# Forming Q from two absolute values of h, in a linear attention with a rational feed-forward layer

## The chip, the cores and the metric

One Trainium2 chip, one of its cores, one launch. The metric is the device time of an execution in microseconds (us). The median of three runs of the kernel before is 860.86 us (860.64 to 860.94).

## The reference

The attention is linear and its output is normalised over each head; the result, laid out as 4608 tokens of 512 features, goes through a feed-forward layer with a rational activation:

```
kv[d, e] = sum over s of k[s, d] * v[s, e]      (8 batches, 8 heads, 576 x 64)
out = q @ kv;  x = out / rms(out) * g_norm                          (4608 x 512)
h   = x @ w_in                                                      (4608 x 2048)
P   = a0 + a1 h + a2 h^2 + a3 h^3
Q   = 1 + |b0| |h| + |b1| h^2
y   = (P / (Q + 1e-6)) @ w_out                                      (4608 x 512)
```

The weights come as 64-bit floats and are taken apart on the chip.

## The kernel before

**Tiling.** The tokens are worked on in nine tiles of 512 (t = 0 to 8), the 2048 hidden features in sixteen chunks of 128 (c = 0 to 15). One pair (t, c) is a slot. In a slot TensorE (PE) makes h of a chunk, 128 x 512, in one PSUM bank (`gemm1`, L493, and L486 in the first four slots), and multiplies the activated chunk of two slots earlier with w_out (`gemm2`, L560, and L553 in the first twelve slots) into four accumulators `acc`. From tile 1 on each product is split in three fp32r matmuls of high and low parts, so a slot has 12 matmuls of `gemm1` and 12 of `gemm2`. Two PSUM banks hold h, and h of slot i+1 is made while slot i is activated.

**Activation of a slot.** It is spread over three engines, each of which runs its list in order. ScalarE (ACT): `v = |b1 h|` (L501), `u = -(a3 h + a2)` (L502), then the high part `gh` of the slot before (L539), the absolute value `q = |q|` (L510), Ln (L513) and Exp (L514), which give the first guess `r` of 1/Q in PSUM. VectorE (DVE): `q = (v + |b0|) h` (L504), `u = u h` (L505), `u = (u - a1) h` (L511), `u = (u - a0) r` (L520), `r = (q + 1 + eps) r` (L521), and the product of the Newton step with the numerator (L529). GpSimd (POOL): the low part `gl` (L540). `h` and `r` lie in PSUM; `v`, `q`, `u`, `gh` and `gl` lie in SBUF. [...]

**What else runs on these engines.** In tile 0 the weights are converted in the gaps: `hi`, `lo` (L209 on ACT, L211 on DVE), `shift` (L232), `or` (L237), `add` (L242, mostly POOL), `cast` (L249) and `rest` (L269). A table `first_tiles` written by hand names the engine, slot and place of each step; the places are points of the slot's code (s, h, q, v, e, r, g, z). From tile 1 on the attention of the next tile runs in fixed slots: `ql` on POOL (L361) in slots 3, 4, 5 and 7, its norm on POOL (L439) in slots 12 and 13, the split of the next x in slot 14 (casts L249 on ACT, low parts L316 on DVE). At the end of a tile `evacuate` copies the accumulators (L567, L569). Slot 15 of tile 8 is done in two halves by `finish`.

**Order.** The instructions are in the order in which the program is written; the framework adds the semaphore waits. It lets one engine at a time use a PSUM bank: L504, which reads h from its bank, comes after both reads of that bank by ACT (L501 and L502).

Of the kernel before, what the change touches and what calls it, by code (L numbers as in the profile page):

```python
# [12 lines left out]
AF = mybir.ActivationFunctionType  # L13
ALU = mybir.AluOpType
# [9 lines left out]
def linear_attention_then_rational_ffn(  # L24
# [10 lines left out]
    PE, ACT, DVE, POOL = nc.tensor, nc.scalar, nc.vector, nc.gpsimd  # L35
# [29 lines left out]
    b0abs = const.tile([P, 1], F32, name="b0abs")  # L65
# [46 lines left out]
    def f32(t):  # L112
        return t.bitcast(F32)
# [134 lines left out]
    def copy(by, to, of):  # L248
        ACT.copy(to, of) if by == ACT else by.tensor_copy(to, of)  # L249
# [222 lines left out]
    def strands(f):  # L472
        return f.rearrange("p (a b) -> p b a", a=2)

    def gemm1(t, c):
        if t == NTILE - 1 and c % 3 == 2:
            ph = ps_at.tile([P, TW], F32, tag="at", name=f"h_{t}_{c}", bufs=1)
        else:
            ph = ps_h.tile([P, TW], F32, tag="h", name=f"h_{t}_{c}")
        gemm1_part(t, c, ph)  # L480
        return ph
# [14 lines left out]
    def ew_a(t, c, ph, w=TW, between=lambda: None):  # L496
        nm = f"{t}_{c}"
        v = work.tile([P, w], F32, tag="d", name=f"v_{nm}")
        q = work.tile([P, w], F32, tag="q", name=f"q_{nm}")
        u = work.tile([P, w], F32, tag="u", name=f"u_{nm}")  # L500
        ACT.activation(v, ph, AF.Abs, scale=b1)  # L501
        ACT.activation(u, ph, AF.Identity, bias=na[:, 2:3], scale=na[:, 3:4])  # L502
        between()
        DVE.scalar_tensor_tensor(q, v, b0abs, ph, ALU.add, ALU.mult)  # L504
        DVE.tensor_tensor(u, u, ph, ALU.mult)  # L505
        pend[t, c] = (q, u)

    def ew_b(t, c, ph, r, between=lambda: None):
        q, u = pend[t, c]
        ACT.activation(q, q, AF.Abs)  # L510
        DVE.scalar_tensor_tensor(u, u, na[:, 1:2], ph, ALU.add, ALU.mult)  # L511
        between()
        ACT.activation(r, q, AF.Ln, bias=bias[:, 2:3], scale=QSC)  # L513
        ACT.activation(r, r, AF.Exp, bias=bias[:, 3:4], scale=-1.0)  # L514
        pend[t, c] = (q, u, r)
# [16 lines left out]
    def ew_d(t, c, w=TW):  # L532
        u = pend.pop((t, c))[1]
        if (t, c) in gs:
            return
        nm = f"{t}_{c}"
        gh = work.tile([P, w], F32R, tag="gh", name=f"gh_{nm}")
        gl = work.tile([P, w], F32R, tag="gl", name=f"gl_{nm}")
        ACT.copy(gh, u)  # L539
        POOL.tensor_tensor(gl, u, f32(gh), ALU.subtract)  # L540
        gs[t, c] = (gh, gl)
# [4 lines left out]
    def gemm2(t, c):  # L546
        g = gs.pop((t, c))
        first, last = c == 0, c == NF - 1
        if first:
            acc[t] = [ps_acc.tile([P, DM], F32, tag="acc", name=f"acc_{t}_{s}") for s in range(NSUB)]  # L550
        if unsplit2(t, c):
            for s in range(NSUB):
                PE.matmul(acc[t][s], g[:, s * P:(s + 1) * P], w32["wo", c], start=first, stop=last)  # L553
            return
        (gh, gl), (wh, wl) = g, whl["wo", c]
        products = (gh, wh), (gh, wl), (gl, wh)
        order = in_turn(behind2.get((t, c)), NSUB)
        for n, (s, j) in enumerate(order):
            a, w = products[j]
            PE.matmul(acc[t][s], a[:, s * P:(s + 1) * P], strands(w) if t else w, start=first and j == 0, stop=last and all(k != s for k, _ in order[n + 1:]))  # L560
# [14 lines left out]
    def finish(t, ph):  # L575
        c = NF - 1
        parts = [slice(k * TW // 2, (k + 1) * TW // 2) for k in range(2)]
        rooms = ("d", 2), ("q", 2), ("u", 2), ("gh", 2), ("gl", 2)
        spare = ("qr", 1), ("qh", 1), ("ql", 1), ("rb", 2), ("rb", 2)
        halves = []  # L580
        for n, tags in enumerate((rooms, spare)):
            new = [work.tile([P, TW // 2], F32 if m < 3 else F32R, tag=tag, name=f"{'vquab'[m]}_last_{n}", bufs=bufs) for m, (tag, bufs) in enumerate(tags)]
            halves.append((*new, ps_at.tile([P, TW // 2], F32, tag=("r", "at")[n], name=f"r_last_{n}", bufs=1)))
        for k, (v, q, u, gh, gl, r) in zip(parts, halves):
            ACT.activation(v, ph[:, k], AF.Abs, scale=b1)
            ACT.activation(u, ph[:, k], AF.Identity, bias=na[:, 2:3], scale=na[:, 3:4])
        ew_d(t, c - 1)
        for k, (v, q, u, gh, gl, r) in zip(parts, halves):
            DVE.scalar_tensor_tensor(q, v, b0abs, ph[:, k], ALU.add, ALU.mult)
            DVE.tensor_tensor(u, u, ph[:, k], ALU.mult)  # L590
            DVE.scalar_tensor_tensor(u, u, na[:, 1:2], ph[:, k], ALU.add, ALU.mult)
            ACT.activation(q, q, AF.Abs)
            ACT.activation(r, q, AF.Ln, bias=bias[:, 2:3], scale=QSC)
            ACT.activation(r, r, AF.Exp, bias=bias[:, 3:4], scale=-1.0)
        gemm2(t, c - 2)
        for v, q, u, gh, gl, r in halves:
            DVE.scalar_tensor_tensor(u, u, na[:, 0:1], r, ALU.add, ALU.mult)
            DVE.scalar_tensor_tensor(r, q, QEPS, r, ALU.add, ALU.mult)
            DVE.scalar_tensor_tensor(u, r, 2.0, u, ALU.subtract, ALU.mult)
            ACT.copy(gh, u)  # L600
            DVE.tensor_tensor(gl, u, f32(gh), ALU.subtract)

        def products(c, gs, order, s0=0):
            wh, wl = whl["wo", c]
            for s, j in order:
                a, w = ((gs[0], wh), (gs[0], wl), (gs[1], wh))[j]
                PE.matmul(acc[t][s], a[:, (s - s0) * P:(s - s0 + 1) * P], strands(w), start=False, stop=c == NF - 1 and j == 2)

        def store(s, by):
            ob = work.tile([P, DM], F32, tag="at", name=f"ob_{t}_{s}", bufs=4)  # L610
            r0 = t * TW + s * P
            if by is not None:
                copy(by, ob, acc[t][s])
                nc.sync.dma_start(out[r0:r0 + P], ob)
                return
            for e, (by, queue) in enumerate(((DVE, nc.sync), (ACT, ACT))):
                es = slice(e * DM // 2, (e + 1) * DM // 2)
                copy(by, ob[:, es], acc[t][s][:, es])
                queue.dma_start(out[r0:r0 + P, es], ob[:, es])

        before = gs[t, c - 1]
        products(c - 1, before, [(s, j) for s in range(2) for j in range(3)])
        products(c, halves[0][3:5], [(s, j) for s in range(2) for j in range(2)] + [(s, 2) for s in range(2)])
        store(0, DVE)
        store(1, ACT)
        for s, by in (2, DVE), (3, None):
            products(c - 1, before, [(s, j) for j in range(3)])
            products(c, halves[1][3:5], [(s, j) for j in range(3)], 2)
            store(s, by)
# [166 lines left out]
    ph = h00  # L796
# [22 lines left out]
    for i, (t, c) in enumerate(slots[:-1]):  # L819
        rest = {0: [], 1: [], 2: []}  # L820
        todo(i, "s")
        ew_a(t, c, ph, between=lambda: todo(i, "h"))
        if i:
            ew_d(*slots[i - 1])
        todo(i, "q")
        ew_b(t, c, ph, r_bank(t, c), lambda: todo(i, "v"))
        todo(i, "e")
        if i >= LAG:
# [3 lines left out]
        if i < 4:  # L832
            ph = gemm1(0, i + 1)
# [13 lines left out]
        if t == NTILE - 1:  # L847
            ahead += [gemm1(*slots[k]) for k in ((i + 1, i + 2) if c == 0 else (i + 2,)) if k < len(slots)]
            ph = ahead.pop(0) if ahead else None
        elif i >= 4:  # L850
            ph = gemm1(*slots[i + 1])
        if c == NF - 2 and 0 < t < NTILE - 1:
            xl = [split(t + 1, p) for p in range(NPAIR)]
            for k in range(2):
                rest[k].append(xl[k])
                rest[2].append(xl[2 + k])
        ew_c(t, c, lambda k: [todo(i, "rgz"[k]), *(f() for f in rest[k])])
    finish(NTILE - 1, ph)


# [42 lines left out]
```

## Time and profile before

| | us |
|---|---|
| median of three runs | 860.86 |
| the profiled execution | 860.87 |
| its span, first to last instruction | 859.1 |
| PE busy | 841.8 (98%) |
| DVE busy | 685.1 (80%) |
| ACT busy | 698.9 (81%) |
| POOL busy | 327.9 (38%) |

The page gives busy time by engine and by line. Matmul ends are modelled, so where a time lost on PE is wanted it is read from the starts: twelve matmuls of 128x512 start 0.216 us apart, 2.59 us together, and what two neighbours lie further apart is lost. The chain of waits tells which work ended last, followed back from the end. The granted TensorE clock is at its full level through the kernel.

### The profile page before, as it was taken

The numbers are of one execution on the slowest core, as the hardware profiler recorded it, in microseconds if no ns is written. First come the engines' busy times: TensorE is split into PE (matmuls) and PEld (weight loads), VectorE is DVE, ScalarE is ACT, GpSimd is POOL, SyncE is SP. The second block draws the span as 40 slices with busy tenths as digits, with TensorE's granted clock in tenths as the row PEclk, the third lists the DMA queues.
The fourth block names the chain that finished last, engine by engine and source line by source line (L and its number), as shares of the span: only waits on it lengthen the run. The fifth ranks groups of instructions, "written<-read, shape, count | busy, mean of one in ns | idle before, by whom it ended". The sixth has DMA issues, their size and how long they took to land.

```text
span 859.1 us, 11993 instructions
## 1 busy us (share of the span) xinstructions
PE 841.8 (98%) x4370; PEld 695.4 (81%) x4370; DVE 685.1 (80%) x1022; ACT 698.9 (81%) x1129; POOL 327.9 (38%) x265
## 2 busy tenths in 40 slices
PE   8999999999999999999999999999999999999997
PEld 5465568888888888888888888888888888888886
DVE  3999999987886788768875897678867877787886
ACT  5999789887798678867886888777887888778875
POOL 3596574434342143324242424233323324242221
PEclk9999999999999999999999999999999999999999
DMA  9683353023020501032113111020202010101001
GB/s 361 276 308 130 127 171 111 26 75 122 2 71 29 169 6 62 26 135 50 49 37 136 50 50 36 15 51 2 74 25 50 2 62 25 43 8 50 1 1 49
DMA packets 24191, 65.93 MB, mean 77 GB/s; under 512 B 2372, under 2 KB 2756, under 8 KB 24132
## 3 DMA queue, kind: packets, MB, share of 16 engines
q1 hardware_dynamic: 23968, 65.04, 22.4%
q8 instruction: 34, 0.56, 0.3%
q14 instruction: 25, 0.20, 0.1%
q10 hardware_dynamic: 164, 0.14, 0.0%
HBM read 55.59 MB, written 9.57 MB: 76 GB/s over the span
## 4 chain that ended last, share of the span: by engine, by line
PE 47%; DVE 26%; ACT 21%; issue 3%; DMA 2%; POOL 1%; ACTq 0%; DVEq 0%; POOLq 0%
PE h L493 21%; PE acc L560 20%; DVE u L520 5%; ACT r L513 5%; ACT q L510 5%; ACT r L514 5%; DVE q L504 5%; DVE r L521 4%; DVE u L529 4%; DVE x L316 2%; DMA raw_wi<-in_w_in_dram 2%; PE ms L344 1%; ACT u L502 1%; ACT v L501 1%; PE op L391 1%
## 5 line engine op out<-in xcount | busy, mean ns | idle before, releaser
L493 PE MATMUL h<-x,wiparts 128*128 128x512 f32 x1680 | 390.1, 382 | 0.2 <-DVE x L316 0.2
L493 PEld LDWEIGHTS h<-x,wiparts 128*128 128x128 f32 x1680 | 315.1, 189 | 50.2 <-issue 3.4
L540 POOL TENSOR_TENSOR gl<-u,gh 128x512 fp32r<-128x512 f32 x131 | 170.7, 1303 | 409.7 <-ACT gh L539 338.5
L520 DVE SCALAR_TENSOR_TENSOR u<-u,na,r 128x512 f32<-128x512 f32 x143 | 106.7, 746 | 82.0 <-ACT r L514 81.7
L504 DVE SCALAR_TENSOR_TENSOR q<-v,b0abs,h 128x512 f32<-128x512 f32 x143 | 106.1, 742 | 53.3 <-ACT u L502 52.6
L501 ACT ACTIVATE v<-h,b 128x512 f32<-128x512 f32 x143 | 98.3, 687 | 48.5 <-PE h L493 46.5
L560 PE MATMUL acc<-woparts,gh 128*128 128x512 f32 x400 | 121.1, 382 | 3.8 <-ACT r L514 2.5
L560 PE MATMUL acc<-woh,gh 128*128 128x512 f32 x320 | 121.3, 379 | 0.0
L560 PE MATMUL acc<-woh,gl 128*128 128x512 f32 x320 | 121.3, 379 | 0.0
L510 ACT ACTIVATE q<-q 128x512 f32<-128x512 f32 x143 | 90.4, 632 | 37.1 <-DVE q L504 35.3
L560 PE MATMUL acc<-wol,gh 128*128 128x512 f32 x320 | 118.9, 379 | 0.4 <-POOL wol L269 0.4
L539 ACT CAST gh<-u 128x512 fp32r<-128x512 f32 x131 | 81.1, 619 | 46.2 <-DVE u L529 46.2
L511 DVE SCALAR_TENSOR_TENSOR u<-u,na,h 128x512 f32<-128x512 f32 x143 | 106.9, 748 | 5.1
L502 ACT ACTIVATE u<-h,na 128x512 f32<-128x512 f32 x143 | 110.9, 776 | 0.0
L513 ACT ACTIVATE r<-q,bias 128x512 f32<-128x512 f32 x143 | 99.1, 693 | 4.5
L521 DVE SCALAR_TENSOR_TENSOR r<-q,r 128x512 f32<-128x512 f32 x143 | 98.5, 689 | 0.0
L514 ACT ACTIVATE r<-r,bias 128x512 f32<-128x512 f32 x143 | 94.7, 662 | 4.6
L505 DVE TENSOR_TENSOR u<-u,h 128x512 f32<-128x512 f32 x143 | 97.4, 681 | 0.0
L529 DVE SCALAR_TENSOR_TENSOR u<-r,u 128x512 f32<-128x512 f32 x131 | 90.5, 691 | 4.2
L560 PEld LDWEIGHTS acc<-woparts,gh 128*128 128x128 f32 x400 | 74.9, 189 | 17.5 <-ACT r L514 4.3
L560 PE MATMUL acc<-woparts,gl 128*128 128x512 f32 x200 | 77.2, 386 | 2.6 <-POOL gl L540 2.5
L560 PEld LDWEIGHTS acc<-wol,gh 128*128 128x128 f32 x320 | 60.5, 189 | 9.3 <-POOL wol L269 0.8
(140 smaller groups left out, 873.4 us busy)
## 6 DMA issues: line engine op xcount, KB each, us to landing
kvm<-in_kv_dram SPq DMA_DIRECT2D x28, 640.0 KB
raw_wo<-in_w_out_dram SPq DMA_DIRECT2D x8, 1024.0 KB
qr<-in_qT_dram SPq DMA_DIRECT2D x32, 256.0 KB
rb<-rd SPq DMA_DIRECT2D x32, 256.0 KB
out_dram<-ob SPq DMA_DIRECT2D x16, 512.0 KB
raw_wi<-in_w_in_dram SPq DMA_DIRECT2D x6, 1024.0 KB
first<-in_first_dram SPq DMA_DIRECT2D x4, 640.0 KB
raw_wi<-in_w_in_dram SPq DMA_DIRECT2D x4, 512.0 KB
```

The lines of the kernel that those rows point to most:

```text
L493: PE.matmul(ph, w, f, start=(n == 0), stop=(n == len(order) - 1))
L502: ACT.activation(u, ph, AF.Identity, bias=na[:, 2:3], scale=na[:, 3:4])
L504: DVE.scalar_tensor_tensor(q, v, b0abs, ph, ALU.add, ALU.mult)
L510: ACT.activation(q, q, AF.Abs)
L511: DVE.scalar_tensor_tensor(u, u, na[:, 1:2], ph, ALU.add, ALU.mult)
L513: ACT.activation(r, q, AF.Ln, bias=bias[:, 2:3], scale=QSC)
L514: ACT.activation(r, r, AF.Exp, bias=bias[:, 3:4], scale=-1.0)
L520: DVE.scalar_tensor_tensor(u, u, na[:, 0:1], r, ALU.add, ALU.mult)
L521: DVE.scalar_tensor_tensor(r, q, QEPS, r, ALU.add, ALU.mult)
L529: DVE.scalar_tensor_tensor(g, r, 2.0, u, ALU.subtract, ALU.mult)
L540: POOL.tensor_tensor(gl, u, f32(gh), ALU.subtract)
L560: PE.matmul(acc[t][s], a[:, s * P:(s + 1) * P], strands(w) if t else w, start=first and j == 0, stop=last and all(k != s for k, _ in order ...
```

## The change

ACT writes `|h|` into `q` straight from the bank of h, as the second of now three reads of that bank; DVE then forms `q = (v + |b0|) |h|` with both operands in SBUF; the absolute value of the quadratic term between DVE's step and Ln is gone. The number of instructions on each engine stays. In the slots:

```diff
         ACT.activation(v, ph, AF.Abs, scale=b1)
+        ACT.activation(q, ph, AF.Abs)
         ACT.activation(u, ph, AF.Identity, bias=na[:, 2:3], scale=na[:, 3:4])
         between()
-        DVE.scalar_tensor_tensor(q, v, b0abs, ph, ALU.add, ALU.mult)
+        DVE.scalar_tensor_tensor(q, v, b0abs, q, ALU.add, ALU.mult)
         DVE.tensor_tensor(u, u, ph, ALU.mult)
         pend[t, c] = (q, u)
 
     def ew_b(t, c, ph, r, between=lambda: None):
         q, u = pend[t, c]
-        ACT.activation(q, q, AF.Abs)
         DVE.scalar_tensor_tensor(u, u, na[:, 1:2], ph, ALU.add, ALU.mult)
```

The same in `finish`, for each half of the last slot:

```diff
             ACT.activation(v, ph[:, k], AF.Abs, scale=b1)
+            ACT.activation(q, ph[:, k], AF.Abs)
             ACT.activation(u, ph[:, k], AF.Identity, bias=na[:, 2:3], scale=na[:, 3:4])
...
-            DVE.scalar_tensor_tensor(q, v, b0abs, ph[:, k], ALU.add, ALU.mult)
+            DVE.scalar_tensor_tensor(q, v, b0abs, q, ALU.add, ALU.mult)
...
-            ACT.activation(q, q, AF.Abs)
```

ACT in slot 1 of tile 4, before (a name is tile of memory, token tile, chunk and a number; `h_4_1` is the bank of h):

```order
L501 ACTIVATE v_4_1_3895<-h_4_1_3879,b1_85 128x512
L502 ACTIVATE u_4_1_3897<-h_4_1_3879,na_83 128x512
L539 CAST gh_4_0_3902<-u_4_0_3853 128x512
L510 ACTIVATE q_4_1_3896<-q_4_1_3896 128x512
L513 ACTIVATE r_4_1_3906<-q_4_1_3896,bias_91 128x512
L514 ACTIVATE r_4_1_3906<-r_4_1_3906,bias_91 128x512
```

and now:

```order
L501 ACTIVATE v_4_1_3895<-h_4_1_3879,b1_85 128x512
L502 ACTIVATE q_4_1_3896<-h_4_1_3879 128x512
L503 ACTIVATE u_4_1_3897<-h_4_1_3879,na_83 128x512
L539 CAST gh_4_0_3903<-u_4_0_3853 128x512
L513 ACTIVATE r_4_1_3907<-q_4_1_3896,bias_91 128x512
L514 ACTIVATE r_4_1_3907<-r_4_1_3907,bias_91 128x512
```

The absolute value moved from behind `gh` to between `v` and `u`; Ln now follows `gh` and waits for DVE's q itself.

DVE from the end of slot 6 to slot 7 of tile 0, before (`wiw`, `wow`, `raw` and `wiparts` are weights under conversion, in SBUF):

```order
L237 SCALAR_TENSOR_TENSOR wiw10_638<-raw_wi10_494,wiw10_638 128x1024
L529 SCALAR_TENSOR_TENSOR g_0_6_673<-r_0_6_633,u_0_6_627 128x512
L504 SCALAR_TENSOR_TENSOR q_0_7_678<-v_0_7_677,b0abs_84,h_0_7_657 128x512
L505 TENSOR_TENSOR u_0_7_679<-u_0_7_679,h_0_7_657 128x512
L511 SCALAR_TENSOR_TENSOR u_0_7_679<-u_0_7_679,na_83,h_0_7_657 128x512
L269 TENSOR_TENSOR wiparts0_675<-wiw0_220,wiparts0_675 128x1024
```

and now:

```order
L237 SCALAR_TENSOR_TENSOR wiw10_638<-raw_wi10_494,wiw10_638 128x1024
L529 SCALAR_TENSOR_TENSOR g_0_6_673<-r_0_6_634,u_0_6_627 128x512
L505 SCALAR_TENSOR_TENSOR q_0_7_678<-v_0_7_677,b0abs_84,q_0_7_678 128x512
L506 TENSOR_TENSOR u_0_7_679<-u_0_7_679,h_0_7_657 128x512
L511 SCALAR_TENSOR_TENSOR u_0_7_679<-u_0_7_679,na_83,h_0_7_657 128x512
L269 TENSOR_TENSOR wiparts0_675<-wiw0_220,wiparts0_675 128x1024
```

Nothing moved on DVE: the second operand of q is in SBUF where it was in PSUM, and the wait for ACT's `u` went from q to the instruction behind it. POOL's list is the same as before.

## Rows read from the trace of the kernel before

**Rows 1.** Busy us by stretch: length, then PE, PEld, DVE, ACT, POOL.
```profile
31.70:134.20 102.50, 98.80 (x480) 61.23 (x479) 99.50 (x129) 92.03 (x141) 69.60 (x43) 1.00 0.50 178
...
204.00:214.00 10.00, 9.62 (x45) 8.12 (x44) 8.37 (x15) 8.12 (x15) 5.57 (x5) 1.00 0.34 91
230.00:240.00 10.00, 9.39 (x43) 7.62 (x42) 9.13 (x15) 8.62 (x14) 2.57 (x2) 1.00 0.07 25
321.00:331.00 10.00, 9.17 (x42) 7.43 (x41) 9.12 (x15) 8.50 (x14) 2.57 (x2) 1.00 0.06 21
...
684.00:694.00 10.00, 8.80 (x40) 7.09 (x39) 8.03 (x12) 8.93 (x16) 2.57 (x2) 1.00 0.05 21
430.00:462.00 32.00, 32.00 (x159) 28.16 (x157) 23.66 (x35) 27.83 (x46) 12.00 (x10) 1.00 0.12 34
```

**Rows 2.** Timeline of PE, tile 4's start and the end: start, us, idle before.
```profile
413.46 0.59 PE L560 MATMUL acc<-woparts,gh 128*128 128x512 f32 x2
414.40 0.48 PE L560 MATMUL acc<-woparts,gl 128*128 128x512 f32 x1 [0.34 <-POOL gl L540]
...
416.66 2.75 PE L493 MATMUL h<-x,wiparts 128*128 128x512 f32 x12
419.90 0.67 PE L560 MATMUL acc<-woparts,gh 128*128 128x512 f32 x2 [0.48 <-ACT r L514]
...
850.81 1.13 PE L607 MATMUL acc<-woparts,a_last 128*128 128x512 f32 x4 [0.36 <-ACT a_last L600]
```

**Rows 3.** The chain that ended last, one slot of that start.
```profile
412.27 0.66 DVE q L504
...
417.12 0.67 DVE q L504
```

**Rows 4.** Groups by line, whole kernel: busy, mean ns | idle before.
```profile
L504 DVE SCALAR_TENSOR_TENSOR q<-v,b0abs,h 128x512 f32<-128x512 f32 x143 | 106.1, 742 | 53.3 <-ACT u L502 52.6
L505 DVE TENSOR_TENSOR u<-u,h 128x512 f32<-128x512 f32 x143 | 97.4, 681 | 0.0
L510 ACT ACTIVATE q<-q 128x512 f32<-128x512 f32 x143 | 90.4, 632 | 37.1 <-DVE q L504 35.3
L394 ACT ACTIVATE sq<-op 128x512 f32<-128x512 f32 x32 | 18.9, 590 | 0.0
```

**Rows 5.** Timeline of DVE and POOL, tile 0, then before tile 4.
```profile
44.42 2.45 DVE L237 SCALAR_TENSOR_TENSOR wiw<-raw_wi,wiw 128x1024 int32<-128x1024 int32 x1
...
43.24 2.37 POOL L269 TENSOR_TENSOR wiparts<-wiw,wiparts 128x1024 fp32r<-128x1024 f32 x1 [1.44 <-ACT wiparts L249]
...
406.13 1.28 DVE L316 TENSOR_TENSOR x<-xf,x 128x512 fp32r<-128x512 f32 x2
...
406.99 1.56 POOL L540 TENSOR_TENSOR gl<-u,gh 128x512 fp32r<-128x512 f32 x1 [5.17 <-ACT gh L539]
```

**Rows 6.** Groups of DVE from 31.7 to 134.2 us; L237's spread.
```profile
L504 DVE SCALAR_TENSOR_TENSOR q<-v,b0abs,h 128x512 f32<-128x512 f32 x15 | 11.2, 746 | 0.8 <-ACT u L502 0.6
...
L237 DVE SCALAR_TENSOR_TENSOR wiw<-raw_wi,wiw 128x1024 int32<-128x1024 int32 x6 | 9.7, 1616 | 0.0
L237 DVE SCALAR_TENSOR_TENSOR wow<-raw_wo,wow 128x1024 int32<-128x1024 int32 x7 | 9.5, 1356 | 0.0
...
L237 DVE SCALAR_TENSOR_TENSOR wow<-raw_wo,wow x8: 1193/1225/1683, 26.1 to 120.8; 128x1024 int32<-128x1024 int32 x8
```

**Rows 7.** Timeline of tile 0: POOL and q, first and last meeting.
```profile
34.38 2.42 POOL L242 TENSOR_TENSOR wiw<-wiw,raw_wi 128x1024 int32<-128x1024 int32 x1 [1.22 <-issue]
...
34.68 0.75 DVE L504 SCALAR_TENSOR_TENSOR q<-v,b0abs,h 128x512 f32<-128x512 f32 x1 [0.43 <-ACT u L502]
...
122.81 2.94 POOL L242 TENSOR_TENSOR wow<-wow,raw_wo 128x1024 int32<-128x1024 int32 x1 [1.56 <-ACT raw_wo L209]
...
125.38 0.74 DVE L504 SCALAR_TENSOR_TENSOR q<-v,b0abs,h 128x512 f32<-128x512 f32 x1
```

**Rows 8.** Waits of PE from 31.7 to 134.2 us.
```profile
PE acc L560 <- POOL gl L540: 1.0, 1, 1.0
```

## The prediction

> **What bounds the kernel now.** I read three views in this order: busy time by stretch, the timeline of PE, and the chain of waits. PE is busy 98% of the span (the table above), and in the middle of a tile it has no gap at all: 32.00 of 32.00 us from 430 to 462 [rows 1]. There the activation has time to spare, and a shorter activation is worth nothing. PE loses time in two kinds of places only.
>
> The first is tile 0, from 31.7 to 134.2 us: DVE is busy 99.5 of 102.5 us, ACT 92.0, POOL 69.6, PE 98.8 [rows 1]. Four engines are nearly full, DVE most of all. What DVE loses there comes out at the end of the stretch, where PE takes up the split product of slot 12 and stands 1.0 us for its low part [rows 8].
>
> The second is the start of each of the tiles 2 to 7, six places. At tile 4 the matmul of 413.46 has a successor due 0.43 us later that starts at 414.40, a loss of 0.51; the twelve from 416.66 end at 419.25 and the next starts at 419.90, a loss of 0.65 [rows 2]. Together 1.16 us, where busy time shows 0.83 (the stretch of tile 3 has 9.17 of 10 like that of tile 4). Adding the same 0.33 to the first (0.61) and the last (1.20) of the six [rows 1] gives 0.94 + 4 x 1.16 + 1.53 = 7.1 us in all. Besides these, 0.4 us go before 214 us [rows 1] and 0.4 at the very end [rows 2]. At a tile's start the chain runs round a loop: DVE's q at 412.27, ACT's absolute value, Ln, Exp, three DVE steps, the next q at 417.12 [rows 3], 4.85 us a slot. PE needs 24 x 0.216 = 5.18, so the loop only catches up slowly with what the split of x has delayed.
>
> **The change part by part.** *ACT.* 143 absolute values of 0.632 us out of SBUF go, as many out of PSUM come. The nearest row without a scale operand that reads PSUM is the square L394, 0.590 [rows 4]. The saving of 143 x 0.04 = 6 us of ACT time lies beside fuller engines; I count nothing.
>
> *The loop.* The new absolute value runs while the previous slot is still on DVE, so a link of 0.632 [rows 4] and a hop between engines, some 0.65, leaves the loop: 4.85 becomes 4.2. DVE's own six steps, at about 0.7 each like the two of [rows 4], need 4.2 as well, so DVE is next and nothing shorter is to be had. In the middle of a tile q gains nothing: v, |h|, then q, Ln takes as long from h as v, u, q, absolute value, Ln did less some 0.1, and PE is the bound.
>
> *What the six starts get back.* The slots before them follow h of PE until slot 14, so the lead at slot 14 is one link, some 0.7 us, not several. Then the operand of q counts. gl of that slot is asked for at 406.99 and the two DVE subtractions L316 run till 407.41; POOL ends at 408.55, 1.56 after its start and 1.14 after L316's end [rows 5]. So an operation of DVE with two SBUF operands and one of POOL do not run at once. The new q, which follows L316, has two SBUF operands too, finds POOL waiting and stands some 1.1 us until gl is done. Of the lead 0.15 is left for the first wait; the next two slots win 0.65 again, which is all of the second wait. So 0.8 of 1.16 comes back, 5.0 of 7.1 over the six, with 3.9 (the second wait alone, 6 x 0.65) and 7.1 as bounds. The 0.4 before 214 and the 0.4 at the end I count as won, since nothing but the loop stands before them: **5.8 us gained from tile 1 on**, between 3.9 and 7.9.
>
> *What tile 0 pays.* The strongest row is L237: two SBUF operands, begun at 44.42 while POOL ran from 43.24 to 45.61, it took 2.45 us [rows 5] where the median is 1.22 [rows 6]. It did nothing until POOL had finished. q with h from PSUM never does that: 15 in this stretch took 0.746 on the mean, as everywhere, under POOL or not [rows 6, 4]. From now on it does. At the places where q stands now it meets a running operation of POOL eight times in this stretch. The first is 34.68 against 34.38 to 36.80, a rest of 2.1; the last is 125.38 against 122.81 to 125.75, a rest of 0.4 [rows 7]; in between the rests are 0.3, 0.6, 1.8, 0.7, 1.2 and 1.2. The sum is 8.3 us. Four more times POOL starts while q runs and is held for half of q's 0.746 on the mean, an estimated 1.5 in all, which the next DVE operation of that kind or PE's weights see. Against this, q no longer waits for u (0.8 [rows 6]), and the loop gives one link of 0.65 in slot 14: 1.5 back. The sum is 8.3 + 1.5 - 1.5 = **8.3 us lost**.
>
> The lower bound is the rate of L237 itself: 6 at 1.616 and 7 at 1.356 are 3.3 us above 13 x 1.22 [rows 6], 0.25 each; 16 q make 4.0, less 1.5 is 2.5. The upper bound adds the meeting of slot 0, before the stretch, an estimated 2.3 us, the longest rest there could be of such an operation: 10.6. I take 8.3, from the row nearest to it, q's own places: L237's successor on POOL is mostly its own consumer, so POOL stands idle when it starts; q has no such relation. Whatever DVE is late at slot 12 PE is late too, since it already stands there [rows 8].
>
> [...]
>
> The sum is made against the profiled execution, 860.87 us (span 859.1), which is also the median: 860.87 + 8.3 - 5.8 = **863.4**.
>
> **The rivals.** *Few meetings.* When q moves, it and POOL may find an order in which they miss each other as L237 mostly does. For it: the median of L237, 1.22 [rows 6], is its lone time. Then 860.87 + 2.5 - 5.8 = 857.6. *Meetings feed each other.* A held POOL operation delivers its weights late, the next DVE step meets the following one, and slot 0 starts it 2.3 us late; at the tile starts only the second wait goes: 860.87 + 10.6 - 3.9 = 867.6. POOL's 69.6 of 102.5 busy speaks for it. *The late activation is covered in tile 0.* PE has 3.7 us of idle there, and some of the delay may fall into it; with 5.8 lost and 5.8 won the time stays at 860.9. Against it: that idle exists because PE waits for the same activation. *The change does what it is written for and q is not held at all.* Then tile 0 wins 1.5, the starts 7.9: 851.5. Only the lack of a row of exactly this form speaks for it.
>
> **How the numbers follow.** A difference of 0.2%, 1.7 us, is about what a measurement of this kernel can tell from none. Chances: forecast 0.47 (861 to 866), few meetings 0.23, feeding each other 0.15, covered 0.10, not held 0.05. Faster takes few meetings nearly whole and not held: 0.27. Same takes covered and the low edge of the forecast: 0.23. Slower is the rest, 0.50. The range of 856.5 to 868.5 leaves out not held, the lower part of few meetings and the upper of feeding: 2 in 10. The likeliest case's own range is 861 to 866.
>
> **What would show it.** Right: in tile 0 q has a mean well above 0.746 with single ones of 2 to 3 us, each ending some 0.7 after a POOL operation; PE reaches the first split product later; in the tile starts the loop is 4.2, L520 waits little for Exp, gl's wait of PE is near 0.35 and the one after it is gone. Wrong: q at 0.74 throughout (then it is not held), or tile 0 of the old length with long q (then PE's slack covered it), or PE's two waits at the tile starts unchanged (then the loop was not what they wait for).

## The result and the profile after

| | before | after |
|---|---|---|
| median, four runs each on one chip (us) | 860.9 (860.64 to 861.31) | 869.28 (868.78 to 869.63) |
| ratio, 95% interval | | 1.0096 (1.0080 to 1.0112) |
| the profiled execution, its span | 860.87, 859.1 | 868.78, 867.0 |

The changed kernel is slower by 1.0%. The forecast had the side (863.4, slower the likeliest) and too little of it; the time lies 0.8 us above its range of 856.5 to 868.5.

The page of after, beside the table of before (span, busy us by engine, the chain that ended last, and the line of q):

```profile
span 867.0 us, 11988 instructions
...
PE 841.9 (97%) x4370; PEld 697.3 (80%) x4370; DVE 712.3 (82%) x1022; ACT 669.0 (77%) x1129; POOL 331.0 (38%) x265
...
PE 75%; DVE 19%; issue 2%; ACT 2%; POOL 1%; DVEq 0%; ACTq 0%; POOLq 0%
...
L505 DVE SCALAR_TENSOR_TENSOR q<-v,b0abs,q 128x512 f32<-128x512 f32 x143 | 127.0, 888 | 81.0 <-ACT q L502 81.0
```

The chain of before:

```profile
PE 47%; DVE 26%; ACT 21%; issue 3%; DMA 2%; POOL 1%; ACTq 0%; DVEq 0%; POOLq 0%
```

ACT lost 29.9 us of busy time and DVE, whose list has not changed by one instruction, gained 27.2. The chain tells that the change did in the tiles what it is for (ACT's share fell from 21% to 2%, PE's rose from 47% to 75%), so the question is where DVE's 27 us lie. q has 20.9 of them (127.0 against 106.1 [rows 4]): 10.2 in tile 0, 7.2 in the slots 15 of seven tiles, 2.8 in four slots of tile 1. A meeting, from here on, is a q that finds an operation of POOL running. What each stage makes of the time is in the next table. The first row gives when PE starts h of a slot before; the others how much later (+) or earlier (-) it starts in another kernel, each in its profiled execution. Between slot 9 of tile 1 and slot 9 of tile 7 lie the six tile starts; the kernels below "after" are the experiments.

| us | (1, 9) | (7, 9) | (8, 15) | end of span |
|---|---|---|---|---|
| before | 183.24 | 728.63 | 841.22 | 859.09 |
| after | +13.09 | +7.44 | +7.44 | +7.90 |
| `tile0_operand` | +16.07 | +16.00 | +16.00 | +16.01 |
| `tile0_order` | +0.54 | +0.49 | +0.49 | +0.49 |
| `late_only` | -0.68 | -6.28 | -6.28 | -5.82 |
| `before_small_add` | -0.85 | -0.88 | -0.88 | -0.88 |
| `after_small_add` | +3.07 | -2.68 | -2.68 | -2.21 |
| `slot0_old` | +13.99 | +8.43 | +8.43 | +8.90 |
| `five_old` | +5.66 | +0.20 | +0.20 | +0.67 |
| `order_late` | -0.91 | -10.01 | -10.01 | -9.54 |
| `late_finish_old` | -1.09 | -6.59 | -6.59 | -7.23 |
| `late_15old` | -0.98 | -9.00 | -9.00 | -9.64 |
| `abs_in_psum` | -0.93 | -10.19 | -10.19 | -10.82 |

So after pays 13.1 us ahead of slot 9 of tile 1, wins 5.65 back at the six starts, and pays 0.46 at the very end. `late_only`, with the old form in tile 0, is 0.68 early at slot 9 of tile 1; so tile 0 by itself pays some 13.8.

**Tile 0.** Groups of DVE's instructions in tile 0 (busy us, mean ns), first after, 26 to 148 us:

```profile
L505 DVE SCALAR_TENSOR_TENSOR q<-v,b0abs,q 128x512 f32<-128x512 f32 x16 | 22.1, 1384 | 0.0
L237 DVE SCALAR_TENSOR_TENSOR wow<-raw_wo,wow 128x1024 int32<-128x1024 int32 x8 | 12.8, 1602 | 0.1
...
L232 DVE TENSOR_SCALAR wow<-raw_wo 128x1024 int32<-128x1024 int32 x8 | 9.5, 1183 | 0.0
...
L237 DVE SCALAR_TENSOR_TENSOR wiw<-raw_wi,wiw 128x1024 int32<-128x1024 int32 x6 | 8.3, 1378 | 0.0
L232 DVE TENSOR_SCALAR wiw<-raw_wi 128x1024 int32<-128x1024 int32 x6 | 6.9, 1149 | 0.0
...
L242 DVE CUSTOM_DVE_ANT_0 wow<-raw_wo,wow 128x2048 uint16<-128x2048 uint16 x1 | 2.2, 2172 | 0.0
```

and the same instructions before, 26 to 135 us:

```profile
L504 DVE SCALAR_TENSOR_TENSOR q<-v,b0abs,h 128x512 f32<-128x512 f32 x16 | 11.9, 745 | 0.8 <-ACT u L502 0.6
...
L237 DVE SCALAR_TENSOR_TENSOR wow<-raw_wo,wow 128x1024 int32<-128x1024 int32 x8 | 10.7, 1340 | 0.1
L237 DVE SCALAR_TENSOR_TENSOR wiw<-raw_wi,wiw 128x1024 int32<-128x1024 int32 x6 | 9.7, 1616 | 0.0
...
L232 DVE TENSOR_SCALAR wow<-raw_wo 128x1024 int32<-128x1024 int32 x8 | 8.2, 1029 | 0.0
L232 DVE TENSOR_SCALAR wiw<-raw_wi 128x1024 int32<-128x1024 int32 x6 | 5.5, 920 | 0.0
...
L242 DVE CUSTOM_DVE_ANT_0 wow<-raw_wo,wow 128x2048 uint16<-128x2048 uint16 x1 | 1.5, 1482 | 0.0
```

q has gained 10.2 us, L232 2.7, L237 0.7 and L242 0.7: 14.3. DVE's waits ahead of slot 15 fell by 1.4 (0.8 for `u`, 0.6 for Exp), which leaves 12.9; q of slot 15 of tile 0 starts at 144.76, where it stood at 131.76. How a single q looks (start, us, [idle before <-releaser]): DVE, POOL and PE of after in slot 0:

```profile
28.07 2.89 DVE L505 SCALAR_TENSOR_TENSOR q<-v,b0abs,q 128x512 f32<-128x512 f32 x1
30.89 0.67 DVE L506 TENSOR_TENSOR u<-u,h 128x512 f32<-128x512 f32 x1
31.66 0.75 DVE L511 SCALAR_TENSOR_TENSOR u<-u,na,h 128x512 f32<-128x512 f32 x1
32.33 1.55 DVE L232 TENSOR_SCALAR wiw<-raw_wi 128x1024 int32<-128x1024 int32 x1
...
27.69 2.73 POOL L242 TENSOR_TENSOR wow<-wow,raw_wo 128x1024 int32<-128x1024 int32 x1 [3.01 <-ACT q L502]
30.36 2.98 POOL L316 TENSOR_TENSOR x<-xf,x 128x512 fp32r<-128x512 f32 x2
...
32.47 3.70 PE L486 MATMUL h<-xf,wiw 128*128 128x512 f32 x8 [2.66 <-DVE u L511]
```

q begins 0.4 us behind the start of POOL's L242, which ends at 30.42; q ends at 30.96 and is 2.89 long instead of 0.74. PE stands 2.66 for the step behind it, where it stood 0.5 before. L232 then begins under POOL's next operation and takes 1.55, where one that met nothing takes 0.69. The sixteen q of tile 0 show long ones in slots 0 (2.89), 2 (2.87), 7 (2.59), 8 (2.63) and 13 (1.75), 0.93 to 1.19 in four more, and 0.72 to 0.75 in the other seven. Each of the nine long ones ends 0.55 behind the end of a POOL operation that was running when it began.

**The tile starts.** Timeline of after at the start of tile 4 (the first pieces lie in slot 15 of tile 3): DVE, POOL, PE.

```profile
416.69 1.28 DVE L316 TENSOR_TENSOR x<-xf,x 128x512 fp32r<-128x512 f32 x2
417.90 1.77 DVE L505 SCALAR_TENSOR_TENSOR q<-v,b0abs,q 128x512 f32<-128x512 f32 x1
...
423.15 0.74 DVE L505 SCALAR_TENSOR_TENSOR q<-v,b0abs,q 128x512 f32<-128x512 f32 x1
...
427.38 0.74 DVE L505 SCALAR_TENSOR_TENSOR q<-v,b0abs,q 128x512 f32<-128x512 f32 x1
...
417.85 1.27 POOL L540 TENSOR_TENSOR gl<-u,gh 128x512 fp32r<-128x512 f32 x1 [4.99 <-ACT gh L539]
...
424.43 0.59 PE L560 MATMUL acc<-woparts,gh 128*128 128x512 f32 x2
425.36 0.48 PE L560 MATMUL acc<-woparts,gl 128*128 128x512 f32 x1 [0.33 <-POOL gl L540]
...
427.62 2.75 PE L493 MATMUL h<-x,wiparts 128*128 128x512 f32 x12
430.21 0.60 PE L560 MATMUL acc<-woparts,gh 128*128 128x512 f32 x2
```

The loop is 4.23 (423.15 to 427.38) instead of 4.85 [rows 3]. The second wait of [rows 2] is gone: 430.21 follows its twelve matmuls without a gap. The first stands nearly as it was, 0.50 lost for 0.51: q of slot 15 finds gl running and takes 1.77, 1.03 too long.

**The end.** The last slot in two halves, after:

```profile
854.57 1.28 POOL L540 TENSOR_TENSOR gl<-u,gh 128x512 fp32r<-128x512 f32 x1 [3.90 <-ACT gh L539]
854.69 1.44 DVE L590 SCALAR_TENSOR_TENSOR q_last<-v_last,b0abs,q_last 128x256 f32<-128x256 f32 x1
...
858.72 1.13 PE L607 MATMUL acc<-woparts,a_last 128*128 128x512 f32 x4 [0.83 <-ACT a_last L600]
```

The second half's q meets gl (1.44; the first half's took 0.47), and PE loses 0.99 from start to start ahead of `a_last`, where it lost 0.52 before.

### The profile page after: what moved, and what is told of

The parts are those of the page before. It is cut to its first block, busy times and chain, and to the rows that moved or that the text cites. A ratio compares the mean times of both kernels' runs of the same rounds, so it can differ in the third digit from the quotient of the medians.

```text
span 867.0 us, 11988 instructions
## 1 busy us (share of the span) xinstructions
PE 841.9 (97%) x4370; PEld 697.3 (80%) x4370; DVE 712.3 (82%) x1022; ACT 669.0 (77%) x1129; POOL 331.0 (38%) x265
## 4 chain that ended last, share of the span: by engine, by line
PE 75%; DVE 19%; issue 2%; ACT 2%; POOL 1%; DVEq 0%; ACTq 0%; POOLq 0%
PE h L493 34%; PE acc L560 33%; DVE q L505 4%; DVE u L520 2%; DVE u L511 2%; DVE x L316 2%; DVE r L521 2%; DVE u L506 2%; PE ms L344 1%; DVE wow L237 1%; DVE u L529 1%; PE op L391 1%; PE op L390 1%; PE acc L553 1%; PE ms L410 1%
## 5 line engine op out<-in xcount | busy, mean ns | idle before, releaser
L493 PE MATMUL h<-x,wiparts 128*128 128x512 f32 x1680 | 390.9, 383 | 1.6 <-ACT r L514 1.6
L493 PEld LDWEIGHTS h<-x,wiparts 128*128 128x128 f32 x1680 | 316.1, 190 | 52.1 <-issue 2.7
L505 DVE SCALAR_TENSOR_TENSOR q<-v,b0abs,q 128x512 f32<-128x512 f32 x143 | 127.0, 888 | 81.0 <-ACT q L502 81.0
L502 ACT ACTIVATE q<-h 128x512 f32<-128x512 f32 x143 | 84.8, 593 | 0.0
```

Source lines behind the costliest of these rows:

```text
L493: PE.matmul(ph, w, f, start=(n == 0), stop=(n == len(order) - 1))
L505: DVE.scalar_tensor_tensor(q, v, b0abs, q, ALU.add, ALU.mult)
```

## The experiments

**Theory:** from now on q has two operands in SBUF and cannot run while POOL works (2.89 for 0.74 in slot 0); that costs in tile 0 and nowhere else but at slot 15 and the last slot. **Rivals:** ScalarE's moved absolute value, which puts casts and conversions of tile 0 later, costs it; or what the starts win is only the catching up of a late tile 0. Line numbers shift by a few in these kernels; names don't. Each ratio in this section is against runs of the kernel before on the same chip (860.57 to 860.59 us).

### The operand alone, in tile 0

```diff
-        DVE.scalar_tensor_tensor(q, v, b0abs, ph, ALU.add, ALU.mult)
+        DVE.scalar_tensor_tensor(q, v, b0abs, ph if t else v, ALU.add, ALU.mult)
```

> The kernel before, with one difference in tile 0: q multiplies by v, in SBUF, where it multiplied by h in PSUM (so Q of tile 0 has another factor); ScalarE's absolute value stays between q and Ln, and no instruction moves. If the place of the operand is what costs in tile 0, the time is 860.9 + 13 = 874, give or take 2, and q of tile 0 shows single ones of 2 to 3 us. If the moved absolute value is what costs (three reads of h ahead of DVE, casts and conversions later on ScalarE), it is 860.9.

875.73 us against 860.59, ratio 1.0175 (1.0162 to 1.0188). Its q of tile 0, and the same group of the next kernel, in which only ScalarE's order is new:

```profile
L504 DVE SCALAR_TENSOR_TENSOR q<-v,b0abs 128x512 f32<-128x512 f32 x16 | 25.5, 1592 | 0.0
```

```profile
L506 DVE SCALAR_TENSOR_TENSOR q<-v,b0abs,h 128x512 f32<-128x512 f32 x16 | 11.9, 746 | 0.3 <-ACT u L504 0.2
```

### ScalarE's order alone, in tile 0

```diff
         ACT.activation(v, ph, AF.Abs, scale=b1)
+        if t == 0:
+            ACT.activation(q, ph, AF.Abs)
...
-        DVE.scalar_tensor_tensor(q, v, b0abs, ph, ALU.add, ALU.mult)
+        DVE.scalar_tensor_tensor(q, v, b0abs, ph, ALU.add, ALU.mult if t else ALU.max)
...
-        ACT.activation(q, q, AF.Abs)
+        if t:
+            ACT.activation(q, q, AF.Abs)
```

> The kernel before, with one difference in tile 0: ScalarE makes the absolute value of h into q between v and u, as in the changed kernel, and none between q and Ln, but VectorE's q still reads h from PSUM (it takes the larger of v + |b0| and h, so that Ln has a positive argument; Q of tile 0 is another). If the operand is what costs, there is nothing to lose here: 860.9, at best 1.5 less for the shorter loop. If the moved absolute value is what costs, 874.

861.22, ratio 1.0007 (0.9998 to 1.0015): no change. The pair settles tile 0: the operand alone costs all of it and more, the order alone nothing that can be told from none.

### The new form from tile 1 on

```diff
-        ACT.activation(q, ph, AF.Abs)
+        if t:
+            ACT.activation(q, ph, AF.Abs)
...
-        DVE.scalar_tensor_tensor(q, v, b0abs, q, ALU.add, ALU.mult)
+        DVE.scalar_tensor_tensor(q, v, b0abs, q if t else ph, ALU.add, ALU.mult)
...
+        if not (t):
+            ACT.activation(q, q, AF.Abs)
```

> The new form of q in tiles 1 to 8 and in the last slot; tile 0 as it was before. The theory (q with two operands in SBUF cannot run beside POOL, and only tile 0 has POOL busy enough for that to cost) puts +13.1 us of the traced delay into tile 0 and -5.2 behind it, so it expects 869.3 - 13.1 = 856.2 us, 4.7 under the kernel before. If what is won at the tile starts is won only because tile 0 ended late (work that had piled up by then is caught up later in any case), it is 860 to 861. If the two stages are independent but the end alone loses 1.2, its tile starts read as in the changed kernel: one wait of 0.5 for gl, none for Exp.

854.67, ratio 0.9931 (0.9920 to 0.9943), 1.5 better than expected. The starts win 5.6 here (-0.68 to -6.28 in the table) as in after (13.09 to 7.44, 5.65), so they owe nothing to a late tile 0. The two parts add up to within 1 us: `tile0_operand` with +15.1 and this with -5.9 make +9.2, and after has +8.4.

### Is it POOL's running operation?

POOL's adds on 32 columns, in either kernel:

```diff
         w = ups[u].bitcast(I32)[:, part]
+        if by == POOL:
+            w, low = w[:, 0:32], low[:, 0:32]
         by.tensor_tensor(w, w, low, ALU.add)
```

> The kernel before with POOL's adds of the weights (L242 on POOL, 34 of its 70 us in tile 0) on 32 columns of 512 or 1024 alone, so the weights lack part of their low word; nothing else is left out and no instruction moves. It is the base line for the next run: the same edit in the changed kernel. By itself it should be some 2 to 4 us under 860.9, since VectorE's L232 and L237, which stand behind such adds in tile 0 (0.69 alone, up to 1.53 beside one), become free.

> The changed kernel with the same edit. Of the 10.2 us by which q of tile 0 is too long, 7.2 stand behind an add of POOL (slots 0, 2, 3, 7, 9, 14), and so do five of the seven long L232. If POOL's running operation is what holds q, the tile 0 loss of 13 falls to 3 or 4 and this kernel is 1 to 2 us under its base line, instead of 8.4 over it; q of slots 0, 2 and 7 is 0.75. If q is slow in tile 0 for another reason (its operand, ScalarE's order, the clock), it stays 8 over the base line.

860.01, ratio 0.9993 (0.9984 to 1.0002), and 859.53, ratio 0.9987 (0.9977 to 0.9996). Of the changed form's 8.4 us -0.5 is left, and up to slot (1, 9) 3.9 of 13.1 (+3.07 less -0.85), as expected. q of slots 0, 2 and 7 is 0.74 to 0.75. But the total came out higher than the 1 to 2 us gain that I named, and the long q are not those that were left over: new ones stand in slots 3, 4 and 6, which had none or a small one (2.32, 2.85 and 1.55), behind POOL's `rest`. POOL and then DVE in slot 4:

```profile
55.79 3.50 POOL L271 TENSOR_TENSOR wiparts<-wiw,wiparts 128x1024 fp32r<-128x1024 f32 x1 [1.69 <-DVE g L531]
...
56.98 2.85 DVE L507 SCALAR_TENSOR_TENSOR q<-v,b0abs,q 128x512 f32<-128x512 f32 x1
```

The first of the two missed: I expected 2 to 4 us from freeing L232 and L237 before, and 0.6 came. From slot 0 to slot 15 DVE's busy time fell by 2.7 us, but its waits for ScalarE, which is busy 92 of 102 us there [rows 1], rose from 1.3 to 3.3. DVE's waits in tile 0 (us, times, longest):

```profile
DVE q L506 <- ACT u L504: 2.0, 4, 0.7
DVE u L522 <- ACT r L516: 1.3, 2, 0.7
```

### Do the meetings stay where they are?

The old form in slot 0 alone, and in the five slots with the longest q:

```diff
-        ACT.activation(q, ph, AF.Abs)
+        if (t or c):
+            ACT.activation(q, ph, AF.Abs)
...
-        DVE.scalar_tensor_tensor(q, v, b0abs, q, ALU.add, ALU.mult)
+        DVE.scalar_tensor_tensor(q, v, b0abs, q if (t or c) else ph, ALU.add, ALU.mult)
```

(the absolute value behind q under the opposite condition; in the second kernel the condition is `t or c not in (0, 2, 7, 8, 13)`).

> The changed kernel with slot 0 of tile 0 alone in the old form. q of slot 0 stood 2.15 us longer than a free one there. If delays simply add, 869.3 - 2.1 = 867.2. If the first late q also sets where the later ones meet POOL, any time between 862 and 869 with other slots held is possible, and the meetings of slots 2, 7, 8 and 13 move or go. If DVE's wait in slot 0 is covered (PE and POOL late anyway), 869.3.

> The changed kernel with the five slots of tile 0 in the old form in which q stood 1.0 to 2.15 us too long (0, 2, 7, 8, 13; 9.0 of the 10.2 in all). If the meetings stay where they were, 869.3 - 9.0 = 860.3 or less. If q meets POOL anew in the slots left, as slot 1 did when slot 0 was in the old form, it stays between 863 and 868, with other long ones among slots 1, 3 to 6, 9 to 12 and 14.

868.12 (862.8 to 869.77 over six runs), ratio 1.0065 (1.0042 to 1.0089), and 861.74 (856.9 to 862.75 over twelve), ratio 1.0005 (0.9992 to 1.0017). In the profiled execution of the first, its slowest (869.77), the long q of slots 2, 7, 8 and 13 are where they were, slot 12 has a new one (1.74), and the meeting has gone from slot 0 to slot 1, with the next add; DVE and POOL:

```profile
34.27 2.87 DVE L506 SCALAR_TENSOR_TENSOR q<-v,b0abs,q 128x512 f32<-128x512 f32 x1 [0.21 <-ACT q L503]
...
34.19 2.41 POOL L242 TENSOR_TENSOR wiw<-wiw,raw_wi 128x1024 int32<-128x1024 int32 x1 [1.22 <-issue]
```

With five slots free, q of tile 0 is 3.0 us too long in all, 2.0 of it this new meeting of slot 1 (2.69); of the 9.0 us by which these five were too long, the time fell by 7.5. So the five were worth most of their price, while slot 0, the only one that was freed by itself, brought 1.2 in the median and nothing in the execution that was traced. Single executions of `slot0_old` differ by 7 us, where those of before differ by 0.8. That other meetings happen in other executions would explain it, but it is not shown: one execution of each kernel was traced.

### What holds the first wait of a tile start, and what the end pays

`order_late`: new order from tile 1 on, q reads h from PSUM. Against `late_only`, one line differs:

```diff
-        DVE.scalar_tensor_tensor(q, v, b0abs, q if t else ph, ALU.add, ALU.mult)
+        DVE.scalar_tensor_tensor(q, v, b0abs, ph, ALU.add, ALU.max if t else ALU.mult)
```

> As the kernel with the new form from tile 1 on (854.7), but VectorE's q of tiles 1 to 8 reads h from PSUM (it takes the larger of v + |b0| and h, so Q is another there); the last slot is in the new form. ScalarE's order is the new one, POOL cannot hold q. The forecast said that the first wait of a tile start (0.5, for gl) stays because q of slot 15 stands 1.1 us behind gl. If so, that wait goes here and the time is 854.7 - 6 x 0.5 = 851.7. If gl is late for another reason (it stands behind the two L316 itself), it is 854.7, within 0.5. If the gain at the tile starts comes from the operand and not from the shorter loop, it is 860.

851.43, ratio 0.9893 (0.9878 to 0.9908), as the forecast's step wants it: with q free of gl the first wait is gone too (a middle start wins 1.43 here, 0.84 in `late_only`). `late_finish_old` is `late_only` with the three lines of `finish` as they were before:

> The new form in tiles 1 to 8, the old one in tile 0 and in the two halves of the last slot. In the changed kernel the matmul of the last chunk comes 7.27 us after the last slot's first activation, where it was 6.40 before: two more reads of h by ScalarE ahead of VectorE, and the second q, 1.44 long, behind gl. If these are what the end loses, 854.7 - 0.9 = 853.8. If PE's end is set by something earlier (h of the last slot comes late now), 854.7.

853.66, ratio 0.9919 (0.9904 to 0.9934); the wait of 0.99 for `a_last` is not there any more, nor is the 0.52 of before. So with the old `finish` the end wins 0.64 against before (-6.59 to -7.23 in the table): the gain that the forecast counted there exists, and the new `finish` costs more than that.

### A version that keeps the gain

Both start from `late_finish_old`. `late_15old` takes the old form also in slot 15 of tiles 1 to 7 (condition `t and c < NF - 1`); `abs_in_psum` keeps the new one there and puts |h| into a PSUM bank that the attention has left:

```diff
+        a = q
+        if 0 < t and c == NF - 1:
+            a = ps_at.tile([P, TW], F32, tag="at", name=f"a_{nm}", bufs=1)
         if t:
-            ACT.activation(q, ph, AF.Abs)
+            ACT.activation(a, ph, AF.Abs)
...
-        DVE.scalar_tensor_tensor(q, v, b0abs, q if t else ph, ALU.add, ALU.mult)
+        DVE.scalar_tensor_tensor(q, v, b0abs, a if t else ph, ALU.add, ALU.mult)
```

> The same with slot 15 of tiles 1 to 7 in the old form: q there is not held (1.03 less), but the absolute value is back between q and Ln (0.63 and a hop). If the two simply add on the way to gl, the wait of 0.48 falls to about 0.1: 853.7 - 2.3 = 851.4. If the old form brings back the old start, with 0.5 and 0.65, 857.

> As the kernel with the new form in tiles 1 to 8 and the old one in tile 0 and the last slot (853.7), but in slot 15 of tiles 1 to 7 ScalarE writes the absolute value of h into the PSUM bank that the attention has left by then; VectorE's q there has one operand in SBUF. All is computed. If gl holding q of slot 15 is what keeps the first wait of a tile start (0.48 each, six of them), it goes: 853.7 - 2.9 = 850.8. If that wait goes only where q reads the bank of h itself, 853.7.

851.38, ratio 0.9892 (0.9879 to 0.9905), and **850.17**, ratio 0.9878 (0.9865 to 0.9891), both as expected to 0.6 us. Slot 15 ahead of tile 4 in `abs_in_psum`, DVE then POOL, and the busy time of PE between 136 and 838 us (length, PE):

```profile
402.65 0.74 DVE L509 SCALAR_TENSOR_TENSOR q<-v,b0abs,a 128x512 f32<-128x512 f32 x1
...
402.63 1.28 POOL L546 TENSOR_TENSOR gl<-u,gh 128x512 fp32r<-128x512 f32 x1 [5.02 <-ACT gh L545]
```

```profile
136.00:838.00 702.00, 702.00 (x3719) 612.86 (x3718) 566.62 (x847) 553.38 (x940) 240.01 (x189) 1.00 0.16 49
```

q begins with gl and still takes 0.74; PE is busy to the last hundredth. By the starts, no two matmuls in this stretch lie more than 0.12 further apart than is due.

## Why the forecast was right in kind and too small

The forecast was 860.87 + 8.3 - 5.8. In the profiled executions it was 860.87 + 13.1 - 5.65 + 0.46 = 868.78. Of the 5.4 between them 4.8 lie ahead of slot 9 of tile 1, and they come from tile 0.

- **The meetings of q, 8.3.** Right in size: q of slots 1 to 15 is 8.05 too long. Not their places: the one at 34.68 did not happen (q of slot 1 took 0.746), nor did that of slot 12; slots 2 and 8 have new ones, and `slot0_old` brought the first back. That the sum was hit so closely with two of eight places wrong is in part luck. A list of places read from before holds as a rate, not as a list.
- **The meeting of slot 0, left out: 2.15.** The first step that failed. It lies before 31.7 us, where I had begun the stretch, and I put it into the upper bound alone with an estimated 2.3. The trace of before had it like the other eight, POOL at work where q stood:

```profile
27.49 2.73 POOL L242 TENSOR_TENSOR wow<-wow,raw_wo 128x1024 int32<-128x1024 int32 x1 [3.02 <-issue]
...
27.88 0.74 DVE L504 SCALAR_TENSOR_TENSOR q<-v,b0abs,h 128x512 f32<-128x512 f32 x1
```

  Nothing covered it: h of slot 2 starts 2.1 us late in after (its wait is 2.66 for 0.5).
- **What others pay, 1.5: measured 4.0 to 4.1.** The second failed step. I counted POOL operations held by q and put half of q's length on each. That part is about right: in slots 5, 10 and 11 POOL's add begins 0.15 to 0.23 behind q and takes 2.77 to 2.83 for 2.41 to 2.42 before. But the add, held back by q, is then longer at work when L232 comes, and L232 waits for it. L232 pays the most, 2.7, and it has one operand in SBUF; I had taken for held only operations with two. The row was there to be had: L232 of `wow` before has a mean of 1.03 where one that meets nothing takes 0.69. Slot 5 in after, POOL and DVE; L232 took 1.17 there before:

```profile
70.58 2.79 POOL L242 TENSOR_TENSOR wiw<-wiw,raw_wi 128x1024 int32<-128x1024 int32 x1 [4.25 <-ACT raw_wi L209]
...
70.36 0.75 DVE L505 SCALAR_TENSOR_TENSOR q<-v,b0abs,q 128x512 f32<-128x512 f32 x1
...
72.41 1.52 DVE L232 TENSOR_SCALAR wow<-raw_wo 128x1024 int32<-128x1024 int32 x1
```

  A delay is passed on in this way. This is the rival "meetings feed each other", to which I gave 0.15; its 867.6 is the nearest of the five, and even it took 10.6 for tile 0.
- **What comes back in tile 0, 1.5.** 1.4 by DVE's waits: right.
- **"Not held", "few meetings", "covered".** q is held, at the full rate, and PE took all of it. The sign that I had named, an end some 0.7 behind a POOL operation, came at 0.55.
- **The six starts and the 0.4 before 214 us, 5.4.** 5.65 measured. The mechanism is shown: the loop of 4.23, the second wait gone, the first kept by q behind gl (`order_late`, `abs_in_psum`). Two sizes in it were off and cancelled: of the first wait I had 0.15 left to win and none was won; a start lost 1.43, not 1.16, since at three places about tile 4's start the successor of a matmul comes another 0.07 to 0.1 late. So 0.84 of 1.43 came back where I had 0.8 of 1.16; `abs_in_psum` wins the 1.43 at each of the middle starts.
- **The end, -0.4: it was +0.46.** The third failed step, a sign. I had the loop alone stand before PE's last wait. In `finish` two more reads of h by ScalarE come ahead of VectorE's steps, and the second q meets the last gl. `late_finish_old` takes both back and gets 1.0; which of the two costs how much no run shows.
- **The operand itself.** q that meets nothing takes 0.74 to 0.75 with both operands in SBUF (the rows of the tile starts above) and 0.742 [rows 4] with h in PSUM: no gain, and the sum of the forecast counts none.

## What to carry to other kernels

Here the move of an operand of a VectorE operation from PSUM to SBUF, beside another one in SBUF, changed its relation to GpSimd (2.89 us under its operation in slot 0) and not its own cost (0.74 to 0.75 alone, for 0.742 before). For such an edit, count GpSimd's busy share where the operation stands, from the first instruction on, and expect its neighbours to pay on top (here 4 us to 10). In this kernel it was best made tile by tile, from tile 1 on and not in tile 0 (854.67 us for 869.28), and in the one slot where both must run by placing the operand in a free PSUM bank (q 0.74 beside gl, 850.17 us). And a meeting that is taken out of one slot can come back in the next, as it did here from slot 0 to slot 1.

## What the runs showed of the hardware

**A one-operand operation is held too.** L232, a shift of 128x1024 int32 from SBUF to SBUF, takes 0.69 by itself. Of the thirteen between q of slot 0 and q of slot 15 in after, one meets nothing. Seven of the other twelve, which begin under an operation of POOL, take 1.47 to 1.55, and five, which find less of it left, 0.81 or 1.11; all twelve end 0.55 to 0.62 behind it (32.33 above). The forecast counted for held only operations with two inputs in SBUF; why L232 is held no run shows. Alone it takes 0.69 where L237, with as many elements and two SBUF inputs, takes 1.22.

**PE's clock fell behind some of its waits.** The granted clock was 0.50 there. Stretches of `tile0_operand`: length, PE, PEld, DVE, ACT, POOL busy, granted clock:

```profile
28.00:32.00 4.00, 1.33 (x4) 0.31 (x3) 3.88 (x4) 1.82 (x4) 4.00 (x3) 1.00 1.02 408
34.00:36.00 2.00, 2.00 (x3) 0.68 (x2) 1.97 (x3) 2.00 (x4) 0.00 (x0) 0.50 0.95 385
98.00:100.00 2.00, 0.00 (x0) 0.00 (x0) 1.97 (x3) 2.00 (x4) 0.00 (x0) 1.00 0.00 0
102.00:104.00 2.00, 2.00 (x8) 1.51 (x5) 2.00 (x3) 1.31 (x3) 2.00 (x2) 0.50 0.00 0
```

Losses of 2.84 and 3.27 us from start to start came ahead of the second and fourth; at 0.50 matmuls that start 0.216 us apart at 1.00 start 0.43 apart (L493 in after, from 100.22 to 102.35 us). A third stretch at 0.50, from 135 to 142 us, came behind losses of 1.59 and 1.19. After shows one such stretch, from 99 to 103 us, behind a loss of 2.30, and none behind the 2.83 of slot 0 or the 2.96 at 131 us. `tile0_operand` has more of such stretches and is 3.0 us later than after at slot (1, 9). Its q alone is 3.3 us longer than after's, which would cover that; what the slower matmuls cost no run here tells apart.

**ScalarE gained five times what the durations said.** I had 143 x 0.04 = 6 us; the page has 29.9 less. Reads of h that stand in a row start before the one ahead has ended, here 0.11 and 0.12 us before. ACT in the first slot of tile 4, after:

```profile
421.01 0.68 ACT L501 ACTIVATE v<-h,b 128x512 f32<-128x512 f32 x1
421.58 0.60 ACT L502 ACTIVATE q<-h 128x512 f32<-128x512 f32 x1
422.06 0.79 ACT L503 ACTIVATE u<-h,na 128x512 f32<-128x512 f32 x1
```

|h| adds 0.48 from its start to the next; the absolute value that it replaces took 0.632 [rows 4], and 143 x 0.15 are 22 of the 29.9. No run here shows what the other 8 are, or any time that ScalarE's gain brought by itself.
